# Adding products on constants to PSUM banks not yet in use, at four places of a linear-attention and mixer kernel

## The chip, the cores and the metric

One core of one Trainium2 chip runs the whole program. The metric is the device time of one execution in microseconds; the median over several executions counts. The engines are called by the names of the profile: PE (TensorE, matrix products and transposes), PEld (its weight loads), ACT (ScalarE), DVE (VectorE), POOL (GpSimd) and SP (SyncE, which issues the DMAs). PSUM is the memory that PE writes its results into; it has eight banks of 512 fp32 columns, and a pool hands them out under a tag.

## The reference

Linear attention over 4 batches of 8 heads, 576 positions, head width 64 and 128 features, then two mixer layers, each with a token mixing and a channel mixing:

```python
def phi(x):
    proj = np.einsum('bhsd,df->bhsf', x, w_phi)
    proj = proj - np.max(np.abs(proj), axis=-1, keepdims=True)
    return np.concatenate([np.exp(proj), np.exp(-proj)], axis=-1)
q_p, k_p = phi(q), phi(k)
kv = np.einsum('bhsf,bhsd->bhfd', k_p, v)
z = np.sum(k_p, axis=2)
num = np.einsum('bhsf,bhfd->bhsd', q_p, kv)
den = np.einsum('bhsf,bhf->bhs', q_p, z)[..., None] + 1e-06
x = (num / den)                     # then as (batch, seq, 512)
# first mixer (rank 32, hidden 2048)
u = x + (x.transpose(0, 2, 1) @ U @ V).transpose(0, 2, 1)
x = u + np.maximum(u @ w_ch1, 0) @ w_ch2
# second mixer (token width 256, hidden 1536)
u = x + (np.maximum(x.transpose(0, 2, 1) @ w_tok1, 0) @ w_tok2).transpose(0, 2, 1)
x = u + np.maximum(u @ w_ch1, 0) @ w_ch2
```

## The kernel before

The work is fp32. Most operands are split into a high part (`..h`) and the rest (`..l`), both in a rounded fp32 format that PE multiplies faster, and a product is the sum of high x high, high x low and low x high. `split` (lines 101 to 103) makes the two parts: one engine casts, another subtracts. The mixer weights come from memory as 64-bit floats; `load64` rebuilds an fp32 tile from the two words with two ACT steps (lines 138, 139) and two DVE steps (lines 141, 144), and `load_half` splits it, for `b` weights with a cast on ACT (`wh_b`, line 94) and a subtraction on POOL (`wl_b`, line 99).

The attention goes over 16 pairs of heads (`g`; four pairs make a batch): projections `pp`, exponentials, the sums over positions into `kvp`, four transposes `kvt` (function `k3`), ACT's cast of them to `KH`, then the products `nm` (function `q2`) of `KH` with the features of q. Pairs 0 to 3 are plain: they don't split q and k features (`g < NF32`). Function `proj` ends with two DVE steps on the projections, `km` and `kd`.

The first token mixing of a batch has three functions. `tm0` makes, for each of five position tiles, four transposes `xp` of the batch's `xT`, splits them to `xh` (ACT) and `xl` (DVE), and sums two products with the constant `US` into one bank, `rp`. `tm1` splits `rp` to `rh` (ACT) and `rl` (DVE). `tm2` makes the eight `mp` products, each of `rh` and of `rl` with the constant `VS`, which DVE adds to `xT` (line 445). After it `ma_u` splits `xT` to `uha` (ACT) and `ula` (DVE), and the first third of the channel mixing follows (`hp_a`, `yp`). The rest of the first channel mixing (`hp_b`, `yb`), the second token mixing of a batch (`tokmix2`: transposes `x2p`, parts `x2h` and `x2l`, sums `gp` with the constants `T1H` and `T1L`) and the second channel mixing (`hp_c`, `yc`) come behind that, with a new set of PSUM pools.

The code names these steps round by round (a table of rounds, `at`), but the order in which each engine gets its instructions is set by the scheduler of the tile framework: it takes the instructions of all engines, runs them against a timeline of its own and emits them in the order in which they come ready there. An engine works its own list strictly in that order; `issue_after(x)` forbids the scheduler to put an instruction ahead of `x`. PSUM pools during the attention and the first third of the first channel mixing: `psk`, one bank (tag `kvp`), `psx`, five banks, `psm`, two banks.

Of the kernel before, what the change touches and what calls it, by code (L numbers as in the profile page):

```python
# [8 lines left out]
F32 = mybir.dt.float32  # L9
# [10 lines left out]
P = 128  # L20
B = 4
# [3 lines left out]
F = 128  # L25
# [3 lines left out]
NT = 5  # L29
N = 288  # L30
# [7 lines left out]

NF32 = 4
WARM = 8  # L40


KQB = 6
# [44 lines left out]
def body(ctx, tc, kq, vd, w_phi, U, V, wm1, wt1, wt2, wm2, out):  # L88
    nc = tc.nc
# [13 lines left out]
        sub(el, lo, src, f32(hi))  # L103

    def mm(o, l, r, start, stop):
        nc.tensor.matmul(o, l, r, start=start, stop=stop, skip_group_check=True)  # L106

    def group(o, pairs, first=True):
        n = len(pairs)
        for i, (l, r) in enumerate(pairs):  # L110
            mm(o, l, r, first and i == 0, i == n - 1)

    cst = ctx.enter_context(tc.tile_pool(name="cst", bufs=1))
    dr = ctx.enter_context(tc.tile_pool(name="dr", bufs=1, space=DRAM))
# [4 lines left out]
    ident = cst.tile([P, P], F32, name="ident")  # L119
# [46 lines left out]
    def w2(w, c):  # L166
        return w[:, C + c * P : C + (c + 1) * P]

    def h_tile(pool, w, uh, ul, name, tag="m"):
        hp = pool.tile([P, 512], F32, tag=tag, name=f"hp_{name}")  # L170
        wh, wl = w
        g = []
        for c in range(NC):
            g += [(w1(wh, c), uh[:, c, :]), (w1(wh, c), ul[:, c, :]), (w1(wl, c), uh[:, c, :])]
        group(hp[:, : uh.shape[2]], g)
        return hp
# [13 lines left out]
    psk = PS.enter_context(tc.tile_pool(name="psk", bufs=1, space=PSUM))  # L190
# [26 lines left out]
    US = ac.tile([P, NT, 4, 32], F32R, name="US")  # L217
    VS = ac.tile([P, S], F32R, name="VS")
# [110 lines left out]
    def k3(g):  # L329
        kvT = a1.tile([P, 2, 2 * F], F32, tag="kvT", name=f"kvT{g}")  # L330
        cp("a", kvT, kvps.pop(g))
        tp = psx.tile([P, 4, P], F32, tag="x", name=f"kvt{g}")
        for j in range(2):
            for s in range(2):
                nc.tensor.transpose(tp[:, 2 * j + s, :], kvT[:, j, s * F : (s + 1) * F], ident)
        if g < NF32:
            KHs[g] = a2.tile([P, 4, P], F32, tag="KH", name=f"KH{g}")
            cp("a", KHs[g], tp)
            return
        KHs[g] = a2.tile([P, 4, P], F32R, tag="KH", name=f"KH{g}")  # L340
        KLs[g] = a2.tile([P, 4, P], F32R, tag="KL", name=f"KL{g}")
        split(tp, KHs[g], KLs[g], "a", "v")

    QT = ((0, 1, 4), (2, 3))
    QS = (slice(0, 320), slice(320, S))

# [23 lines left out]
    def q2(g, j, ch):  # L370
        nm = f"{g}_{j}_{ch}"
        n = QS[ch].stop - QS[ch].start
        eh, el = qe.pop((g, j, ch))
        ps = psx.tile([P, 512], F32, tag="x", name=f"nm{nm}")
        gr = [(KHs[g][:, 2 * j + s], eh[:, s]) for s in range(2)]
        if el is not None:
            gr += [(KLs[g][:, 2 * j + s], eh[:, s]) for s in range(2)]
            gr += [(KHs[g][:, 2 * j + s], el[:, s]) for s in range(2)]
        group(ps[:, :n], gr)
        if ch == 0:  # L380
            nds[g, j] = a1.tile([P, S], F32, tag=f"nd{j}", name=f"nd{g}_{j}")
        cp("a", nds[g, j][:, QS[ch]], ps[:, :n])
# [27 lines left out]
            for j, rows in enumerate((slice(0, D), slice(D, P))):  # L410
                nc.vector.tensor_mul(xTs[b][rows, hp, :], nds.pop((g, j))[rows], rec[rows])

    rps = {}

    def tm0(b, t):
        xT = xTs[b]
        if t == 0:
            rps[b] = psx.tile([P, C], F32, tag="x", name=f"rp{b}")
        rp = rps[b]
        r = P if t < 4 else D  # L420
        xp = psx.tile([P, C], F32, tag="x", name=f"xp{b}_{t}")
        for c in range(NC):
            nc.tensor.transpose(xp[:r, c * P : (c + 1) * P], xT[:, c, t * P : t * P + r], ident)
        xh = at2.tile([P, C], F32R, tag="xh", name=f"xh{b}_{t}")
        xl = at2.tile([P, C], F32R, tag="xl", name=f"xl{b}_{t}")
        split(xp[:r], xh[:r], xl[:r], "a", "v")
        us = US[:r, t].rearrange("p a r -> p (a r)")
        mm(rp, us, xh[:r], t == 0, False)
        mm(rp, us, xl[:r], False, t == NT - 1)

    def tm1(b):
        rh = at2.tile([P, C], F32R, tag="xh", name=f"rh{b}")
# [4 lines left out]
    def tm2(b, ch):  # L437
        rh, rl = rps[b]
        sl = slice(ch * N, (ch + 1) * N)
        xT = xTs[b]  # L440
        for c in range(NC):
            mp = psx.tile([P, 512], F32, tag="x", name=f"mp{b}_{ch}_{c}")
            cs = slice(c * P, (c + 1) * P)
            group(mp[:, :N], [(rh[:, cs], VS[:, sl]), (rl[:, cs], VS[:, sl])])
            nc.vector.tensor_add(xT[:, c, sl], mp[:, :N], xT[:, c, sl])
        nc.sync.dma_start(uD[2 * b + ch], xT[:, :, sl])

# [11 lines left out]
    wA = []  # L459
# [7 lines left out]
    uhl, hss = {}, {}  # L467
# [5 lines left out]
    def ma_h(b, ch, f):  # L473
        nm = f"a{b}_{ch}_{f}"
        pool, tag = (psx, "x") if b == B - 1 and f % 2 else (psm, "m")
        hp = h_tile(pool, wA[f], *uhl[b, ch], nm, tag)
        hh, hl = h_pair(f, nm)
        relu_split(hp[:, :N], hh, hl)
        hss[b, ch].append((hh, hl))
# [15 lines left out]
    for g in range(B * NPAIR):  # L495
        r = 5 * g
# [11 lines left out]
        for i in range(4):  # L508
            j, ch = i % 2, i // 2
# [67 lines left out]
    def tokmix2(b, x2):  # L577
        gp = [psg.tile([P, C], F32, tag=f"g{j}", name=f"gp{b}_{j}") for j in range(2)]
        for t in range(NT):
            r = P if t < 4 else D  # L580
            xp = psh.tile([P, C], F32, tag="m", name=f"x2p{b}_{t}")
            for c in range(NC):
                nc.tensor.transpose(xp[:r, c * P : (c + 1) * P], x2[:, c, t * P : t * P + r], ident)
            xh = b2.tile([P, C], F32R, tag="xh", name=f"x2h{b}_{t}")
            xl = b2.tile([P, C], F32R, tag="xl", name=f"x2l{b}_{t}")
            split(xp[:r], xh[:r], xl[:r], "a", "v")
# [125 lines left out]
```

## Time and profile before

| | us |
|---|---|
| median of 3 executions | 1081.95 |
| lowest, highest | 1081.44, 1084.78 |
| the profiled execution: own time | 1085.54 |
| its span (first to last instruction) | 1083.7 |
| PE busy | 1039.0 (96% of the span) |
| DVE, ACT, POOL busy | 575.2, 420.7, 226.2 |
| mean granted clock of PE, 1 being full | 0.983 |

The profiled execution is one of its own, beside the three. PE's share says that little of the span is left without a product or transpose; it doesn't say that they ran at full clock. The granted clock is therefore read with it, stretch by stretch. The stage of the last batch's token mixing lies at about 372 to 393 us, that of the plain pairs before 85, the second token mixing of the last batch at about 756 to 775.

### The profile page before, as it was taken

The page shows a single profiled execution, that of the slowest core. Times are in us where ns is not written, and L with a number is a line of the kernel's source. Part 1 is how long each engine was busy: PE and PEld are TensorE (multiplying, and loading weights), DVE is VectorE, ACT ScalarE, POOL GpSimd, SP SyncE. Part 2 cuts the span into 40 slices and gives each one's busy share as a digit, 9 for nine tenths or more (in the row PEclk, how much of TensorE's full clock was granted, in tenths as well). Part 3 has the DMA queues.
Part 4 walks back from the last instruction along what each step waited for, and adds up shares of the span by engine and source line. Part 5 has one row for each costly group of instructions (what it writes and reads, how often), then busy time and mean ns, then how long its engine had stood idle before and what let it go on. Part 6 is the DMA issues. An engine that isn't in the chain of part 4 may idle for free.

```text
span 1083.7 us, 16492 instructions
## 1 busy us (share of the span) xinstructions
PE 1039.0 (96%) x6528; PEld 945.5 (87%) x6528; DVE 575.2 (53%) x973; ACT 420.7 (39%) x953; POOL 226.2 (21%) x174
## 2 busy tenths in 40 slices
PE   8978899899989989999999999999999999999998
PEld 6757799789879879999999999999898888888886
DVE  6788987898898588743223223339941121211211
ACT  6676666665665477532112112127621111111110
POOL 3225565554545244200000000003200000000000
PEclk9998999999999969999999999999999999999999
DMA  7552313232220397520200200216401020020101
GB/s 213 151 150 66 97 56 92 75 92 71 75 83 16 110 304 230 176 79 22 88 23 22 88 22 23 88 39 202 150 23 60 1 77 1 1 77 1 39 1 38
DMA packets 59614, 87.36 MB, mean 81 GB/s; under 512 B 14353, under 2 KB 46353, under 8 KB 59537
## 3 DMA queue, kind: packets, MB, share of 16 engines
q1 hardware_dynamic: 59536, 86.32, 25.0%
q8 instruction: 51, 0.84, 0.3%
q14 instruction: 27, 0.21, 0.1%
HBM read 67.27 MB, written 18.95 MB: 80 GB/s over the span
## 4 chain that ended last, share of the span: by engine, by line
PE 79%; DVE 10%; ACT 4%; issue 3%; DMA 3%; POOL 1%; SPq 0%; DVEq 0%; POOLq 0%; ACTq 0%
PE hp_c L106 14%; PE yc L106 14%; PE yb L106 12%; PE hp_b L106 12%; PE hp_a L106 4%; PE pp L106 4%; PE yp L106 4%; PE kvp L106 3%; PE nm L106 3%; PE gp L106 3%; PE m2p L106 2%; PE dT L354 1%; DMA raw_a<-in_wm_dram 1%; DVE km L286 1%; POOL wl_b L99 1%
## 5 line engine op out<-in xcount | busy, mean ns | idle before, releaser
L180 DVE SCALAR_TENSOR_TENSOR hlc<-hp_c,hhc 128x504 fp32r<-128x504 f32 (+1 forms) x60 | 38.2, 636 | 225.4 <-ACT hhc L179 225.4
L179 ACT ACTIVATE hhc<-hp_c 128x504 fp32r<-128x504 f32 (+1 forms) x60 | 33.3, 556 | 247.8 <-PE hp_c L106 247.8
L180 DVE SCALAR_TENSOR_TENSOR hlb<-hp_b,hhb 128x288 fp32r<-128x288 f32 x88 | 40.1, 455 | 160.2 <-ACT hhb L179 160.2
L179 ACT ACTIVATE hhb<-hp_b 128x288 fp32r<-128x288 f32 x88 | 35.9, 408 | 198.2 <-PE hp_b L106 197.8
L106 PE MATMUL hp_b<-ulb,wh_b 128*128 128x288 f32 x352 | 104.0, 296 | 0.0
L106 PE MATMUL hp_b<-uhb,wl_b 128*128 128x288 f32 x352 | 104.0, 296 | 0.0
L106 PE MATMUL hp_b<-uhb,wh_b 128*128 128x288 f32 x352 | 103.8, 296 | 0.0
L106 PE MATMUL yb<-hlb,wh_b 128*128 128x288 f32 x352 | 97.4, 297 | 0.2 <-DVE hlb L180 0.2
L106 PE MATMUL yb<-hhb,wl_b 128*128 128x288 f32 x352 | 97.0, 295 | 0.0
L106 PE MATMUL hp_c<-ulc,wh_c 128*128 128x504 f32 (+1 forms) x240 | 89.1, 371 | 0.0
L106 PE MATMUL hp_c<-uhc,wl_c 128*128 128x504 f32 (+1 forms) x240 | 89.1, 371 | 0.0
L106 PE MATMUL hp_c<-uhc,wh_c 128*128 128x504 f32 (+1 forms) x240 | 88.5, 371 | 0.0
L106 PE MATMUL yc<-hlc,wh_c 128*128 128x504 f32 (+1 forms) x240 | 88.3, 371 | 0.0
L106 PE MATMUL yc<-hhc,wl_c 128*128 128x504 f32 (+1 forms) x240 | 88.1, 370 | 0.0
L99 POOL TENSOR_TENSOR wl_c<-w_c,wh_c 128x512 fp32r<-128x512 f32 x12 | 19.1, 1592 | 327.4 <-ACT wh_c L94 318.3
L99 POOL TENSOR_TENSOR qel<-qe,qeh 128x640 fp32r<-128x640 f32 (+1 forms) x48 | 71.5, 1501 | 26.5 <-ACT qeh L94 13.0
L106 PE MATMUL yc<-hhc,wh_c 128*128 128x504 f32 (+1 forms) x240 | 75.7, 371 | 0.0
L106 PE MATMUL yb<-hhb,wh_b 128*128 128x288 f32 x352 | 67.3, 296 | 1.6 <-ACT hhb L179 1.6
L106 PEld LDWEIGHTS hp_b<-uhb,wh_b 128*128 128x128 f32 x352 | 66.0, 188 | 1.2 <-PE gp L106 1.1
L106 PEld LDWEIGHTS yb<-hlb,wh_b 128*128 128x128 f32 x352 | 66.1, 188 | 1.0 <-DVE hlb L180 0.7
L106 PEld LDWEIGHTS hp_b<-ulb,wh_b 128*128 128x128 f32 x352 | 66.3, 188 | 0.1
L106 PEld LDWEIGHTS yb<-hhb,wl_b 128*128 128x128 f32 x352 | 66.3, 188 | 0.0
(181 smaller groups left out, 2793.1 us busy)
## 6 DMA issues: line engine op xcount, KB each, us to landing
raw_c<-in_wm_dram SPq DMA_DIRECT2D x24, 512.0 KB, 4.3
raw_b<-in_wm_dram SPq DMA_DIRECT2D x22, 512.0 KB, 5.1
kq<-in_kq_dram SPq DMA_DIRECT2D x80, 128.0 KB, 2.1
raw_a<-in_wm_dram SPq DMA_DIRECT2D x10, 512.0 KB, 4.4
rec<-rD SPq DMA_DIRECT2D x32, 144.0 KB, 3.1
uD<-xT SPq DMA_DIRECT2D x8, 576.0 KB, 3.5
sD<-xT SPq DMA_DIRECT2D x8, 576.0 KB, 4.7
ub<-uD SPq DMA_DIRECT2D x8, 576.0 KB, 3.7
```

The lines of the kernel that those rows point to most:

```text
L99: return ENG[e].tensor_tensor(out=o, in0=a, in1=b, op=ALU.subtract)
L106: nc.tensor.matmul(o, l, r, start=start, stop=stop, skip_group_check=True)
L179: nc.scalar.activation(hh, hp, AF.Relu)
L180: nc.vector.scalar_tensor_tensor(out=hl, in0=hp, scalar=0.0, in1=f32(hh), op0=ALU.max, op1=ALU.subtract)
L286: nc.vector.tensor_reduce(out=m, in_=pv, op=ALU.max, axis=AX.X, apply_absolute_value=True)
L354: nc.tensor.transpose(tp[:, o : o + r], ds["q", g, t][:r, j, :], ident[:r, :r])
```

## The change

A new helper, `keep(o, n, behind, r)`, issues n products of 128 x 128 columns of a constant on its own 512 columns (`US`, or `T1H`), all into PSUM tile `o`, and the scheduler may not put them ahead of the instruction `behind`. The result is read by no one: the first real product into the same bank overwrites it. There are 48 of them: 10 into the bank of the first `nm` of pair 3, behind the last `kvt` transpose; 6 into `mp0_0_0` and 6 into `mp3_0_0`, behind the batch's last `rp` product; 8, 2, 2, 2 and 2 into a bank of their own (`spare`, in the pool `psk`, whose bank is free by then), behind the five groups of transposes `xp3_t` of batch 3; 5 into the first `hp_a` of batch 3, behind its last `mp` product; 5 into `gp3_0`, behind the first `x2p` transposes of batch 3.

```diff
+KEEP_X = (8, 2, 2, 2, 2)
+KEEP_M = 6
+KEEP_U = 5
+KEEP_Q = 10
+KEEP_G = 5
     def mm(o, l, r, start, stop):
-        nc.tensor.matmul(o, l, r, start=start, stop=stop, skip_group_check=True)
-
-    def group(o, pairs, first=True):
+        return nc.tensor.matmul(o, l, r, start=start, stop=stop, skip_group_check=True)
+
+    def keep(o, n, behind, r=None):
+        r = US.rearrange("p t a r -> p (t a r)") if r is None else r
+        with tc.issue_after(behind):
+            for i in range(n):
+                mm(o, r[:, :P], r[:, :512], i == 0, i == n - 1)
+
+    def group(o, pairs, first=True, last=True):
...
         hp = pool.tile([P, 512], F32, tag=tag, name=f"hp_{name}")
+        if behind is not None:
+            keep(hp, KEEP_U, behind)
...
-                nc.tensor.transpose(tp[:, 2 * j + s, :], kvT[:, j, s * F : (s + 1) * F], ident)
+                kvl[g] = nc.tensor.transpose(tp[:, 2 * j + s, :], kvT[:, j, s * F : (s + 1) * F], ident).ins
...
         ps = psx.tile([P, 512], F32, tag="x", name=f"nm{nm}")
+        if g == NF32 - 1 and j == 0 and ch == 0:
+            keep(ps, KEEP_Q, kvl[g])
...
             rps[b] = psx.tile([P, C], F32, tag="x", name=f"rp{b}")
+            if b == B - 1:
+                spare.append(psk.tile([P, 512], F32, tag="kvp", name="spare"))
...
+        if b == B - 1:
+            keep(spare[0], KEEP_X[t], last)
...
-        mm(rp, us, xl[:r], False, t == NT - 1)
+        rpl[b] = mm(rp, us, xl[:r], False, t == NT - 1).ins
...
-            group(mp[:, :N], [(rh[:, cs], VS[:, sl]), (rl[:, cs], VS[:, sl])])
+            if c == 0 and ch == 0 and b in (0, B - 1):
+                keep(mp, KEEP_M, rpl[b])
+            group(mp[:, :N], [(rh[:, cs], VS[:, sl])], last=False)
+            mps[b] = mm(mp[:, :N], rl[:, cs], VS[:, sl], False, True).ins
...
-        hp = h_tile(pool, wA[f], *uhl[b, ch], nm, tag)
+        hp = h_tile(pool, wA[f], *uhl[b, ch], nm, tag, mps[b] if b == B - 1 and ch == 0 and f == 0 else None)
...
+            if b == B - 1 and t == 0:
+                keep(gp[0], KEEP_G, last, T1H.rearrange("p t j -> p (t j)"))
```

Since the scheduler works on all instructions at once, the added ones also change the order of others: on every engine from about the first `mp` products of batch 0 on to the middle of batch 1's attention (pairs 6 to 9 and the first channel mixing of batch 0 change places), and again in the stage of batch 3's token mixing. Up to pair 3's products the orders agree, and so they do between those stretches but for the numbers.

PE at the end of pair 3, before (the kernel's tile names with a running number; `x4` is four in a row):

```order
L335 MATMUL kvt3_840<-ident_77,kvT3_838 128x128 x4
L106 MATMUL nm3_0_0_847<-qf3_0_0_786,KH3_845 128x320 x2
L106 MATMUL nm3_1_0_852<-qf3_1_0_793,KH3_845 128x320 x2
L106 MATMUL pp4_1_861<-KWH_132,xgh4_1_857 128x256
L106 MATMUL pp4_1_861<-KWL_133,xgh4_1_857 128x256
```

and after (line 112 is the former 106, 349 the former 335):

```order
L349 MATMUL kvt3_840<-ident_77,kvT3_838 128x128 x4
L112 MATMUL nm3_0_0_847<-US_144 128x512 x10
L112 MATMUL nm3_0_0_847<-qf3_0_0_786,KH3_845 128x320 x2
L112 MATMUL nm3_1_0_862<-qf3_1_0_793,KH3_845 128x320 x2
L112 MATMUL pp4_1_871<-KWH_132,xgh4_1_867 128x256
```

Ten products have come between the transposes and the first `nm`; nothing else moved there.

PE in the token mixing of batch 3, behind the last product of `yp2_1_3`, before:

```order
L106 MATMUL rp3_4939<-xh3_0_4945,US_144 128x512
L423 MATMUL xp3_1_4951<-ident_77,xT3_4285 128x128 x4
L423 MATMUL xp3_2_4980<-ident_77,xT3_4285 128x128 x4
L423 MATMUL xp3_3_4991<-ident_77,xT3_4285 128x128 x4
L106 MATMUL rp3_4939<-xl3_0_4946,US_144 128x512
L423 MATMUL xp3_4_5002<-ident_77,xT3_4285 64x128 x4
L106 MATMUL rp3_4939<-xh3_1_4956,US_144 128x512
```

and after:

```order
L112 MATMUL rp3_4955<-xh3_0_4970,US_144 128x512
L442 MATMUL xp3_1_4976<-ident_77,xT3_4301 128x128 x4
L112 MATMUL spare_4956<-US_144 128x512
L112 MATMUL rp3_4955<-xl3_0_4971,US_144 128x512
L112 MATMUL spare_4956<-US_144 128x512
L442 MATMUL xp3_2_5007<-ident_77,xT3_4301 128x128 x4
L112 MATMUL spare_4956<-US_144 128x512 x2
L442 MATMUL xp3_3_5020<-ident_77,xT3_4301 128x128 x4
L112 MATMUL spare_4956<-US_144 128x512 x2
L442 MATMUL xp3_4_5033<-ident_77,xT3_4301 64x128 x4
L112 MATMUL spare_4956<-US_144 128x512 x2
L112 MATMUL rp3_4955<-xh3_1_4983,US_144 128x512
```

The small groups have come between the transposes; the eight of the first group stand further ahead, before the fifteen products of `yp2_1_3`. The six stand behind the last `rp` product, the five behind the last `mp` product, with nothing between them and the real products of their bank.

DVE in the same stage (lines 141 and 144 are the two steps of the weight conversion, 153 and 156 after; line 99, or 105, is the subtraction of a split), before:

```order
L141 SCALAR_TENSOR_TENSOR w_b0_1_5568<-w_b0_1_5568,r_b0_1_5569 128x512
L99 TENSOR_TENSOR xl3_1_4957<-xp3_1_4951,xh3_1_4956 128x512
L144 SCALAR_TENSOR_TENSOR w_b0_1_5568<-raw_b0_1_5566,w_b0_1_5568 128x512
L99 TENSOR_TENSOR xl3_2_4986<-xp3_2_4980,xh3_2_4985 128x512
L99 TENSOR_TENSOR xl3_3_4997<-xp3_3_4991,xh3_3_4996 128x512
L141 SCALAR_TENSOR_TENSOR w_b1_0_5580<-w_b1_0_5580,r_b1_0_5581 128x512
L99 TENSOR_TENSOR xl3_4_5008<-xp3_4_5002,xh3_4_5007 64x512
L144 SCALAR_TENSOR_TENSOR w_b1_0_5580<-raw_b1_0_5578,w_b1_0_5580 128x512
L141 SCALAR_TENSOR_TENSOR w_b1_1_5590<-w_b1_1_5590,r_b1_1_5591 128x512
L99 TENSOR_TENSOR rl3_5018<-rp3_4939,rh3_5017 128x512
```

and after:

```order
L105 TENSOR_TENSOR xl3_1_4984<-xp3_1_4976,xh3_1_4983 128x512
L153 SCALAR_TENSOR_TENSOR w_b1_0_5624<-w_b1_0_5624,r_b1_0_5625 128x512
L105 TENSOR_TENSOR xl3_2_5015<-xp3_2_5007,xh3_2_5014 128x512
L156 SCALAR_TENSOR_TENSOR w_b1_0_5624<-raw_b1_0_5622,w_b1_0_5624 128x512
L153 SCALAR_TENSOR_TENSOR w_b1_1_5634<-w_b1_1_5634,r_b1_1_5635 128x512
L156 SCALAR_TENSOR_TENSOR w_b1_1_5634<-raw_b1_1_5632,w_b1_1_5634 128x512
L105 TENSOR_TENSOR xl3_3_5028<-xp3_3_5020,xh3_3_5027 128x512
L105 TENSOR_TENSOR xl3_4_5041<-xp3_4_5033,xh3_4_5040 64x512
L153 SCALAR_TENSOR_TENSOR w_b2_0_5646<-w_b2_0_5646,r_b2_0_5647 128x512
L105 TENSOR_TENSOR rl3_5051<-rp3_4955,rh3_5050 128x512
```

Weight steps have moved ahead of the splits: `rl3` had the first step of `w_b1_1` before it, and has the first of `w_b2_0` now. From the first step of `w_b0_0` up to `ula3_0` DVE's list has ten weight steps before and thirteen after. On ACT the casts `xh3_3` and `xh3_4` stand behind `wh_b1_0` after, ahead of it before; on DVE, in the second token mixing of batch 3, `x2l3_0` stands ahead of the first two additions into `x2` and not behind them, and the first steps of `w_c7` ahead of `x2l3_1`, the second ones ahead of `x2l3_2`.

## Rows read from the trace of the kernel before

Times are microseconds; PE, DVE and so on are the engines. In the timelines a row is one instruction, or several alike in a row (x4), and the brackets hold the idle time of the engine just before it and who ended that.

**Rows 1.** The cores: span in us, mean granted clock of PE.

```profile
core 0: 1083.7 us, clock 0.983
```

**Rows 2.** The page: shares of the chain that ended last, by engine.

```profile
PE 79%; DVE 10%; ACT 4%; issue 3%; DMA 3%; POOL 1%; SPq 0%; DVEq 0%; POOLq 0%; ACTq 0%
```

**Rows 3.** Ten-us windows: busy us (instructions) of PE, PEld, DVE, ACT, POOL; PEclk; DMA.

```profile
70.00:80.00 10.00, 6.13 (x26) 4.19 (x25) 8.04 (x15) 6.54 (x17) 1.47 (x1) 0.86 0.58 166
90.00:100.00 10.00, 8.02 (x42) 7.72 (x43) 6.27 (x12) 4.53 (x13) 8.78 (x7) 0.66 0.30 86
380.00:390.00 10.00, 7.79 (x22) 5.32 (x23) 9.72 (x15) 7.28 (x12) 3.85 (x3) 0.55 0.80 270
390.00:400.00 10.00, 8.08 (x40) 7.73 (x41) 8.44 (x12) 6.65 (x12) 4.40 (x3) 0.60 1.02 336
760.00:770.00 10.00, 8.05 (x35) 6.25 (x34) 9.18 (x17) 6.24 (x11) 1.88 (x2) 0.83 0.41 138
```

**Rows 4.** PE timeline, pair 3: start, us, then line, tiles, count, wait before.

```profile
76.27 3.81 PE L106 MATMUL nm<-qf,KH 128*128 128x320 f32 x8 [3.34 <-ACT KH L94]
```

**Rows 5.** Window behind pair 3, columns as in rows 3.

```profile
76.70:83.50 6.80, 6.80 (x30) 5.42 (x29) 6.74 (x10) 3.25 (x9) 3.11 (x2) 0.75 0.58 174
```

**Rows 6.** DVE timeline behind that window.

```profile
84.00 1.40 DVE L286 TENSOR_REDUCE km<-pp 128x4 f32<-128x512 f32 x2 [0.49 <-PE pp L106]
```

**Rows 7.** PE timeline, token mixing of batch 0.

```profile
110.85 0.39 PE L106 MATMUL rp<-xl,US 128*128 128x512 f32 x1
111.08 0.39 PE L106 MATMUL rp<-xh,US 128*128 128x512 f32 x1
...
122.52 0.40 PE L106 MATMUL mp<-VS,rh 128*128 128x288 f32 x1 [2.20 <-DVE xT L445]
```

**Rows 8.** PE timeline, token mixing of batch 3.

```profile
375.40 0.51 PE L106 MATMUL rp<-xh,US 128*128 128x512 f32 x1 [0.81 <-ACT xh L94]
...
380.99 0.63 PE L106 MATMUL rp<-xh,US 128*128 128x512 f32 x1
381.42 0.63 PE L106 MATMUL rp<-xl,US 128*128 128x512 f32 x1
...
384.65 1.33 PE L106 MATMUL mp<-VS,rh 128*128 128x288 f32 x4 [0.68 <-ACT rh L94]
...
389.72 1.33 PE L106 MATMUL hp_a<-uha,wh_a 128*128 128x288 f32 x4 [0.47 <-ACT uha L94]
392.97 0.61 PE L106 MATMUL hp_a<-ula,wh_a 128*128 128x288 f32 x1 [1.92 <-DVE ula L99]
```

**Rows 9.** Window in the token mixing of batch 3, columns as in rows 3.

```profile
380.60:393.00 12.40, 8.87 (x26) 6.05 (x26) 12.12 (x19) 9.06 (x15) 4.40 (x4) 0.51 0.83 265
```

**Rows 10.** Windows of batch 3's hp_a products alone, columns as in rows 3 (no POOL).

```profile
393.00:398.00 5.00, 5.00 (x21) 5.00 (x22) 0.28 (x1) 0.40 (x1) 0.50 1.03 345
398.00:400.50 2.50, 2.50 (x21) 2.50 (x21) 0.17 (x1) 0.40 (x1) 1.00 1.07 410
```

**Rows 11.** DVE timeline, token mixing of batch 3.

```profile
376.11 0.68 DVE L144 SCALAR_TENSOR_TENSOR w_b<-raw_b,w_b 128x512 int32<-128x512 int32 x1
376.71 0.45 DVE L491 TENSOR_TENSOR xT<-yp,xT 128x288 f32<-128x288 f32 x1
...
378.28 1.69 DVE L144 SCALAR_TENSOR_TENSOR w_b<-raw_b,w_b 128x512 int32<-128x512 int32 x1
...
385.24 1.79 DVE L144 SCALAR_TENSOR_TENSOR w_b<-raw_b,w_b 128x512 int32<-128x512 int32 x1
```

**Rows 12.** POOL timeline, same stage.

```profile
378.15 1.28 POOL L99 TENSOR_TENSOR wl_b<-w_b,wh_b 128x512 fp32r<-128x512 f32 x1 [17.93 <-ACT wh_b L94]
```

**Rows 13.** PE timeline, second token mixing of batch 3.

```profile
756.97 0.79 PE L106 MATMUL yb<-hhb,wh_b 128*128 128x288 f32 x4 [0.45 <-ACT hhb L179]
...
762.26 0.50 PE L106 MATMUL gp<-x2l,T1H 128*128 128x512 f32 x1 [1.95 <-DVE x2l L99]
```

**Rows 14.** DVE timeline, same stage.

```profile
760.80 0.81 DVE L573 TENSOR_TENSOR x<-yb,x 128x288 f32<-128x288 f32 x2
```

More of the change, by code (lines that the diff above doesn't have):

```diff
@@ L105, in mm @@
     def mm(o, l, r, start, stop):
-        nc.tensor.matmul(o, l, r, start=start, stop=stop, skip_group_check=True)
-    def group(o, pairs, first=True):
+        return nc.tensor.matmul(o, l, r, start=start, stop=stop, skip_group_check=True)
[5 more added lines that the diff above has]
+    def group(o, pairs, first=True, last=True):
         n = len(pairs)
         for i, (l, r) in enumerate(pairs):
-            mm(o, l, r, first and i == 0, i == n - 1)
+            mm(o, l, r, first and i == 0, last and i == n - 1)
     cst = ctx.enter_context(tc.tile_pool(name="cst", bufs=1))
@@ L167, in w2, with h_tile @@
         return w[:, C + c * P : C + (c + 1) * P]
-    def h_tile(pool, w, uh, ul, name, tag="m"):
+    def h_tile(pool, w, uh, ul, name, tag="m", behind=None):
         hp = pool.tile([P, 512], F32, tag=tag, name=f"hp_{name}")
+        if behind is not None:
+            keep(hp, KEEP_U, behind)
         wh, wl = w
@@ L342, in k3 @@
         split(tp, KHs[g], KLs[g], "a", "v")
+    kvl = {}
     QT = ((0, 1, 4), (2, 3))
@@ L411, in x1 @@
                 nc.vector.tensor_mul(xTs[b][rows, hp, :], nds.pop((g, j))[rows], rec[rows])
-    rps = {}
+    rps, rpl, mps, spare = {}, {}, {}, []
     def tm0(b, t):
@@ L422, in tm0 @@
         for c in range(NC):
-            nc.tensor.transpose(xp[:r, c * P : (c + 1) * P], xT[:, c, t * P : t * P + r], ident)
+            last = nc.tensor.transpose(xp[:r, c * P : (c + 1) * P], xT[:, c, t * P : t * P + r], ident).ins
+        if b == B - 1:
+            keep(spare[0], KEEP_X[t], last)
         xh = at2.tile([P, C], F32R, tag="xh", name=f"xh{b}_{t}")
@@ L582, in tokmix2 @@
             for c in range(NC):
-                nc.tensor.transpose(xp[:r, c * P : (c + 1) * P], x2[:, c, t * P : t * P + r], ident)
+                last = nc.tensor.transpose(xp[:r, c * P : (c + 1) * P], x2[:, c, t * P : t * P + r], ident).ins
+            if b == B - 1 and t == 0:
+                keep(gp[0], KEEP_G, last, T1H.rearrange("p t j -> p (t j)"))
             xh = b2.tile([P, C], F32R, tag="xh", name=f"x2h{b}_{t}")
```

## Prediction, made before the changed kernel was run

> **What bounds the kernel now.** I read the cores first, then the chain, then the windows, then the timeline of the places that the change touches. The mean granted clock is 0.983 over a span of 1083.7 us [rows 1]: if every stretch below full speed were repaired, and TensorE (PE) set the end in all of them, that would give (1 - 0.983) x 1083.7 = 18.4 us, the ceiling for any change of this kind. The chain that ended last is PE for 79%, VectorE (DVE) for 10% [rows 2]: PE's work is on the path nearly everywhere, but some of it hands over to DVE. The windows show where PE is neither full nor at full clock [rows 3]: 70 to 80 us (0.86), 90 to 100 (0.66), 380 to 400 (0.55 and 0.60) and 760 to 770 (0.83). The change has products for the first, the third and the fourth; none stands before 90 to 100, whose 3.4 us at the most I leave as they are. A granted 0.50 is the lower of the two levels, 1.2 GHz instead of 2.4.
>
> So the question for each place is not whether PE gets busier, but two others: does the clock then stay at its upper level, and is PE what the next stage waits for.
>
> **A. Pair 3 (ten products).** PE waits 3.34 us for ScalarE's KH, then runs eight products at 76.27 in 3.81 us [rows 4]. Ten products of 512 columns at the spacing of the rp rows at full clock, 111.08 - 110.85 = 0.23 us [rows 7], are 2.3 us: they fit into the 3.34 and delay nothing. If the clock then stays up, the eight nm products take half of 3.81 and PE is 1.9 us earlier. Who uses that? DVE is busy for 6.74 of the 6.80 us from 76.7 on [rows 5], and PE's next projections need DVE's splits; DVE's first wait on PE after that is 0.49 us at 84.00 [rows 6]. What an earlier PE can give DVE is that 0.49. I take -0.5, bounds 0 (the clock falls all the same, or DVE stays full) and -1.9.
>
> **B. Batch 0 (six products) and what the scheduler made of it.** Six products stand ahead of mp0_0_0, 6 x 0.23 = 1.4 us, and the first real one needs only rh, long there. That delay is taken up behind it: after the first mp group PE waits 2.20 us for a DVE addition [rows 7]. More exposed is that between here and about 215 us all engines' orders changed: products of pairs 6 to 9 and of the first channel mix changed places. The trace of before cannot show what new waits that makes. I bound it by the one wait next to it, gone or once more: -2.2 to +2.2. The moved operations are the same ones, so I take 0.
>
> **C. Batch 3 (27 products, and DVE's order).** This is the largest term. From 380.6 to 393 DVE is busy 12.12 of 12.40 us [rows 9], and what ends the stage is DVE: at 392.97 PE waits 1.92 us for ula [rows 8]. The order shows ten steps of the weight conversion on DVE between the first, of w_b0_0, and ula before, and thirteen after. One that meets nothing lasts 0.68 and takes 0.60 of DVE's time (376.11 to the next at 376.71) [rows 11]. Three more are 3 x 0.60 = +1.8 us for ula. They are taken out of later work that DVE does beside a full PE, so nothing comes back for them.
>
> Against it stands the clock. The first 21 products of hp_a take 5.00 us at 0.50, the next 21 take 2.50 at 1.00 [rows 10]. In before the clock was down from about 381 on [rows 3], while PE waited 0.68 for rh, 0.47 for uha and 1.92 for ula [rows 8]; it rose at 398, after PE had worked from 393 without a gap [rows 10]. Now eight products fill the wait of 0.81 at 375.40, eight more stand between the transposes, six before mp, five before hp_a. The rp products still wait for xl as before, and the order puts xh3_3 and xh3_4 on ScalarE behind one more weight cast, so I expect the clock to fall near 381 again: nothing of the change fills that wait. But then six and five products at the half clock's spacing, 381.42 - 380.99 = 0.43 us [rows 8], are 2.6 and 2.2 us, and with the sixteen mp products between them PE works nearly without a gap from about 384 until ula comes. That is what it had done before the clock rose at 398, so I take the clock as up again when hp_a's row starts: -2.5. The 2.6 us ahead of mp cost little: DVE at that time works off weight steps. C is +1.8 - 2.5 = -0.7. Its ends: -2.5 if the three steps cost nothing, because DVE loses less to stalls; and upwards 3 x 1.79 = +5.4, with no gain from the clock, at the duration of the stalled step of 385.24 [rows 11].
>
> How likely that end is, rows tell too: the step at 378.28 lasted 1.69 instead of 0.68, having started 0.13 us behind GpSimd's wl_b of 1.28 us [rows 11, 12]. The Trainium skill has a rule for this, in SBUF - State Buffer, section "SBUF: two separate sides": DVE and GpSimd share a pair of ports as an exclusive lock, and the one that starts first holds it for its whole instruction (a DVE operation counts if it reads two operands from SBUF and GpSimd reads SBUF too). The rows agree with it: 1.28 - 0.13 + 0.60 is 1.75, and the step took 1.69. By that rule weight steps that are pulled into this stretch pull GpSimd's steps after them and are to be priced as stalled; the sum for C would then be +5.4 in place of -0.7.
>
> **D. Second token mixing, batch 3 (five products).** Behind x2p's transposes PE waits 0.45 us for hhb; five products are 5 x 0.23 = 1.15, so yb starts 0.7 us later. That lies ahead of a wait of 1.95 us for x2l at 762.26 [rows 13], which takes it up. x2l now stands on DVE ahead of the two additions that begin at 760.80 and last 0.81 together [rows 14], so it comes some 0.7 us sooner, while the next two x2l stand behind weight steps that stood after them. I take -0.6. If the clock also holds behind it, (1 - 0.83) x 10 = 1.7 us of the window come back [rows 3]: -1.7. If neither helps, +0.7.
>
> **The sum.** A -0.5, B 0, C -0.7, D -0.6: -1.8 us. The profiled execution took 1085.54 us, its span 1083.7 and 1.8 us around it; -1.8 makes 1083.7. The median of the three runs, 1081.95, lies 3.6 us below it, and the same difference on the median gives **1080.2 us**.
>
> **The rivals.**
> - The clock holds at all three places, and DVE has room: A -1.9, C -2.5, D -1.7, together -6.1, **1075.9 us**. For it: nothing but missing products keeps PE idle at pair 3 and in front of mp and hp_a. Against it: DVE is full at both places [rows 5, 9], and a PE that finishes earlier there only waits longer for DVE.
> - DVE's stalls in batch 3 decide: each of the three added weight steps meets a GpSimd step and lasts 1.79, the clock doesn't return before hp_a, since a later ula only makes PE wait longer. C is +5.4, the sum -0.5 + 5.4 - 0.6 = +4.3, **1086.3 us**, slower. It decides from the point where the three steps last more than (3.2 + 1.1) / 3 = 1.4 us each on average. For it: two of the ten steps lasted 1.69 and 1.79 [rows 11]. Against it: not every step can meet one, as GpSimd has one step for two of DVE's. This is the rival that the Trainium skill's rule of the exclusive lock leads to.
> - The products don't do what they are said to: the clock falls where it fell and comes back as late as before, and they stand ahead of work that is ready: 6 x 0.23 = 1.4 at mp0; in batch 3 8 x 0.23 - 0.81 = 1.0, 1.4 - 0.68 = 0.7 and DVE's 1.8; 1.15 - 0.45 = 0.7 at x2p. Together +5.6, **1087.6 us**. Against it: three of these have a wait behind them that swallows them.
>
> **How the numbers follow.** 0.3% is 3.2 us, about what a measurement of this kernel can tell from no change; the three runs of before spread over 3.3 us. The forecast (-1.8, with its terms free to move by some 3 us, 1078.7 to 1085.2) has 0.43, the first rival 0.35, the second 0.17 (with new waits in pairs 6 to 9, term B, in it), the third 0.05. Faster 0.35, same 0.43, slower 0.22. Both signs hold much, so the likeliest case's own range is 1078.7 to 1085.2; the range for 8 in 10 reaches to the first rival and just to the second: 1075.5 to 1086.5.
>
> **What would show it.** In the profile after: a granted clock near 1.00 in 76 to 81 us but DVE still full there, and a DVE that starts the split of ula some 2 us later than before, with thirteen weight steps ahead of it (C's cost); hp_a's first 21 products in 2.5 us instead of 5.00 (C's gain); weight steps of 1.7 us and more there speak for the second rival. The wait for x2l at 762.26 shorter than 1.95 shows D. The forecast is wrong if the clock stays up all through 375 to 398 and ula comes no later than before (first rival), or if it is down until 398 again (second or third); and B is wrong if PE's waits between 120 and 215 us in sum differ by more than 2.2 us.

## The result, and the profile after

| | before | after |
|---|---|---|
| median, us (executions) | 1081.44 (5) | 1088.58 (5) |
| lowest, highest | 1079.17, 1084.78 | 1085.66, 1091.89 |
| ratio to before, 95% interval | | 1.0067 [1.0045, 1.0089] |
| the profiled execution: own time, mean granted clock | 1085.54, 0.983 | 1085.66, 0.994 |

The changed kernel is slower by 0.67%, some 7 us. The forecast was 1080.2 us, and the measured time lies outside the range, above it. Here and below a loss in us is (ratio - 1) x 1082.

The cores and two lines of the page (busy time of the engines; the chain that ended last) say what the change did and didn't do:

```profile
core 0: 1083.9 us, clock 0.994
```

```profile
PE 1043.7 (96%) x6576; PEld 947.9 (87%) x6576; DVE 582.0 (54%) x973; ACT 420.7 (39%) x953; POOL 228.4 (21%) x174
...
PE 77%; DVE 12%; DMA 4%; issue 3%; ACT 2%; POOL 1%; SPq 0%; DVEq 0%; ACTq 0%; POOLq 0%
```

The clock was granted nearly everywhere, 0.994 against 0.983 [rows 1]. But DVE's share of the chain rose from 10% [rows 2] to 12%, and its 973 instructions, as many as before, took 582.0 us in place of 575.2. Both profiled executions are single ones and took the same time although the medians differ by 7 us: the one of before was a long one of its kind and the one of after the shortest of five. They are therefore compared by stretch. Windows of the changed kernel, columns as in rows 3:

```profile
70.00:80.00 10.00, 8.68 (x54) 7.31 (x52) 9.59 (x16) 6.26 (x20) 2.96 (x2) 1.00 0.49 162
90.00:100.00 10.00, 7.76 (x58) 6.89 (x57) 9.72 (x14) 7.17 (x21) 6.05 (x5) 1.00 0.23 67
380.00:390.00 10.00, 8.37 (x32) 6.59 (x31) 7.85 (x15) 6.71 (x10) 1.93 (x3) 0.75 0.70 239
390.00:400.00 10.00, 8.78 (x62) 8.31 (x62) 8.87 (x9) 5.61 (x12) 5.00 (x4) 1.00 1.00 360
400.00:410.00 10.00, 9.43 (x57) 9.20 (x58) 9.89 (x13) 7.09 (x14) 4.12 (x3) 0.83 0.51 187
760.00:770.00 10.00, 7.44 (x33) 4.91 (x33) 9.97 (x18) 6.54 (x11) 1.76 (x2) 1.00 0.41 144
```

Against [rows 3]: the clock is up in 70 to 80, 390 to 400 and 760 to 770, and half up in 380 to 390. It was also up in 90 to 100, where nothing had been put, and it was down in 400 to 410, where it had not been. What the stretches hand on is told by starts of the same instruction in two traces: the first `rp` of batch 3 began 5.4 us earlier after than before (369.97, 375.40), the first product of `hp_b` 0.25 us later. So whatever was ahead by 370 us had gone by 427. Much of that lead is no gain of the change: by pair 3's transposes, before the first added product, it was 4.9 us already (67.38, 72.27), from one execution to another. Some 3 us of that arose near 38 us, where PE waited 2.64 us for an exponential of ScalarE in the one and 1.20 in the other, and the eight products behind it took 3.64 us at the lower clock and 1.99 at the upper.

### The profile page after: what moved, and what is told of

The parts are those of the page before. It is cut to its first block, busy times and chain, and to the rows that moved or that the text cites. A ratio compares the mean times of both kernels' runs of the same rounds, so it can differ in the third digit from the quotient of the medians.

```text
span 1083.9 us, 16586 instructions
## 1 busy us (share of the span) xinstructions
PE 1043.7 (96%) x6576; PEld 947.9 (87%) x6576; DVE 582.0 (54%) x973; ACT 420.7 (39%) x953; POOL 228.4 (21%) x174
## 4 chain that ended last, share of the span: by engine, by line
PE 77%; DVE 12%; DMA 4%; issue 3%; ACT 2%; POOL 1%; SPq 0%; DVEq 0%; ACTq 0%; POOLq 0%
PE hp_c L112 14%; PE yc L112 14%; PE hp_b L112 12%; PE yb L112 12%; PE yp L112 5%; PE hp_a L112 4%; PE pp L112 3%; PE kvp L112 3%; PE m2p L112 2%; PE nm L112 2%; PE gp L112 2%; PE dT L369 1%; DVE xT L428 1%; DVE km L300 1%; DMA raw_b<-in_wm_dram 1%
```

## The experiments

Sixteen runs, each in five rounds beside the kernel before.

### Which of the four places

Each of the first four kernels keeps the added products of one place and drops the others, as in the first:

```diff
-        if b == B - 1:
-            keep(spare[0], KEEP_X[t], last)
...
-            if c == 0 and ch == 0 and b in (0, B - 1):
+            if c == 0 and ch == 0 and b in ():
...
-            if b == B - 1 and t == 0:
-                keep(gp[0], KEEP_G, last, T1H.rearrange("p t j -> p (t j)"))
```

Pair 3:

> The kernel before with the ten products of pair 3 alone; the order of all other instructions is that of before. The prediction's step A: -0.5 us (0 to -1.9). If the loss of the changed kernel came from the attention's part, this or the next kernel would have to be slower by several us; the traces say it isn't, so 1079 to 1083, within 0.3% of before.

Batch 0:

> The kernel before with the six products ahead of batch 0's first mp alone; with them the scheduler changes the order of all engines in pairs 6 to 9, as in the changed kernel. Theory O (the loss lies in batch 3's stage): no change, within 2 us of before. Rival theory B (the new order of pairs 6 to 9 costs): +3 us or more.

Batch 3:

> The kernel before with the 27 products of batch 3's token mixing alone; DVE's and ScalarE's order in that stage is that of the changed kernel (thirteen weight steps ahead of ula). In the two traces the changed kernel loses 6.2 us between 349 and 427 us. Theory O: the whole loss is here, +5 to +7 us. Rival theory B: less than +3 us.

Second token mixing:

> The kernel before with the five products of the last second token mixing alone, with the order that they bring. The two traces differ by 0.26 us there: +0.3 us, at the most 1 us to either side. The prediction's step D said -0.6.

| kernel | ratio [95%] | us |
|---|---|---|
| pair 3 alone | 0.9987 [0.9970, 1.0004] | -1.4 |
| batch 0 alone | 1.0025 [1.0010, 1.0040] | +2.7 |
| batch 3 alone | 1.0064 [1.0040, 1.0087] | +6.9 |
| second token mixing alone | 1.0012 [0.9996, 1.0027] | +1.3 |

Batch 3 carries the loss, batch 0 a smaller one. Batch 0's alone is no clean number for its own place: with it the scheduler changed the order of the `hp_a` stage of batch 3 as well, which took 1.0 us longer in its trace than before.

### The products or the order

Two things came with the change: products, and a new order on every engine. They can be parted: a table, made from the built program of before or of the changed kernel, pins every engine's list to that order (an issue order, no wait). The kernels of this and the next two sections have this edit and differ in the table, and in whether the products are in.

```diff
+ORDER = "..."
+def fix_order(tc, kept, first):
...
+    for eng, steps in json.loads(zlib.decompress(base64.b85decode(ORDER))).items():
...
+                if prev is not None:
+                    tc.add_manual_dep(i, prev.name, NoSync, reason="order")
+                prev = i
```

Products of batch 3, old order:

> The 27 products of batch 3's token mixing alone, as in the third kernel, but every engine's list of instructions is pinned to that of the kernel before, and the products stand directly behind the instruction that they were put behind. Theory O (the new order of DVE and ScalarE costs the time, the products none): no loss, -3 to +1 us against before. Theory P (the products stand in the way of ready ones, six of them at half clock ahead of mp: 2.7 us in the trace): +2 to +4 us.

New order, no products:

> The kernel before without any added product, with every engine's list pinned to the order of the changed kernel. Theory O: it carries the whole loss and more, +7 to +10 us, since nothing holds the clock. Theory P: +3 us or less.

All products, old order:

> All 48 products, every engine's list pinned to the order of before (batch 0's six stand directly ahead of their bank's first real product). Theory O: faster than before, -1 to -6 us, with the gain of pair 3 (-2.3 measured alone) in it. Theory P: +1 to +4 us.

The last of them once more:

> All 48 products with every engine's list pinned to the order of before, once more, since its gain of 0.2% lay close to what can be told: -1 to -4 us against before again if it is one.

| kernel | ratio [95%] | us |
|---|---|---|
| batch 3's products, old order | 1.0002 [0.9984, 1.0021] | +0.2 |
| new order, no products | 1.0079 [1.0060, 1.0098] | +8.5 |
| all products, old order | 0.9980 [0.9965, 0.9995] | -2.2 |
| the same again | 0.9991 [0.9970, 1.0011] | -1.0 |

This settles the main question. **The order alone costs as much as the whole change (+8.5 [+6.5, +10.6] and +7.2 [+4.9, +9.6] us), and the products in the old order cost nothing**; they gain a little, the first time clear of noise, the second time not. Starts in the traces, against the starts before (375.40, 384.65 and 392.97 in [rows 8]), show where:

| start, less the start before | after | products of batch 3, old order | order alone | all products, old order |
|---|---|---|---|---|
| first `rp` of batch 3 | -5.43 | +0.50 | -0.90 | -5.52 |
| first `mp` | -1.77 | +2.86 | +1.30 | -3.46 |
| first product with `ula` | -2.52 | +1.51 | +1.52 | -5.09 |
| first `hp_b` | +0.25 | +1.47 | +4.59 | -5.14 |

From the first `rp` to `ula` the changed kernel loses 2.9 us, the order alone 2.4, the kernels in the old order 1.0 and 0.4. From `ula` to `hp_b` it is 2.8 and 3.1, and the kernels in the old order neither lose nor gain there: 33.73 and 33.72 us, before 33.77.

### Which part of the order

> No added products. The order of the changed kernel up to the last batch's first transposes (pairs 6 to 9 with the first channel mixing of batch 0), the order of before from there on. In the trace of the order alone this stretch loses 3.2 us between 119 and 209 us, in that of the changed kernel 1.8: +2 to +3 us. If the loss of that stretch was chance: within 1 us.

> No added products. The order of the changed kernel in batch 3's token mixing alone, from the first split up to ula (thirteen weight steps on DVE ahead of it, casts of weights ahead of xh on ScalarE); the order of before elsewhere. The prediction's price of the three steps: +1.8 us; by the trace of the order alone +2.4. If ula's delay is made good behind it: 0.

> No added products. The order of before up to ula of batch 3, that of the changed kernel from there to the start of hp_b (weight steps among the splits of hp_a); nothing of that was priced in the prediction. By the trace of the order alone +3.1 us. If only ula's delay counts: 0.

| new order only in (no products) | ratio [95%] | us |
|---|---|---|
| pairs 6 to 9 | 1.0009 [0.9992, 1.0026] | +1.0 |
| batch 3 up to `ula` | 1.0033 [1.0012, 1.0055] | +3.6 |
| batch 3 behind `ula` | 1.0062 [1.0039, 1.0084] | +6.7 |

The three add up to more than the order alone (8.5), within their intervals, and the last two overlap. The kernel with the new order behind `ula` alone has the ten weight steps of before ahead of `ula`, so the three that the changed kernel does there stand behind it: six weight steps between `ula` and the first split `hla` of `hp_a`, where before has four and the changed kernel three. From the first product with `ula` to the first of `hp_b` its trace has 40.8 us, the changed kernel's 36.5, before's 33.8. So +6.7 is not the price of this stretch in the changed kernel; there it is the 2.8 to 3.1 us above.

Behind `ula` PE had been dense before. PE there, in the kernel with the new order behind `ula` alone, and beside it the rows of DVE and ScalarE that the wait of 2.14 us goes back to:

```profile
402.34 0.40 PE L138 MATMUL hp_a<-uha,wh_a 128*128 128x288 f32 x1 [2.14 <-DVE hla L213]
```

```profile
399.55 0.69 DVE L174 SCALAR_TENSOR_TENSOR w_b<-w_b,r_b 128x512 int32<-128x512 int32 x1 [1.88 <-ACT w_b L171]
400.27 1.65 DVE L177 SCALAR_TENSOR_TENSOR w_b<-raw_b,w_b 128x512 int32<-128x512 int32 x1
401.84 0.45 DVE L213 SCALAR_TENSOR_TENSOR hla<-hp_a,hha 128x288 fp32r<-128x288 f32 x1
```

```profile
398.85 0.67 ACT L171 ACTIVATE w_b<-raw_b 128x512 f32<-128x512 f32 x1 [1.76 <-POOL wl_b L131]
...
400.84 0.39 ACT L212 ACTIVATE hha<-hp_a 128x288 fp32r<-128x288 f32 x1
```

The split that PE waits for, `hla`, takes 0.45 us on DVE at 401.84. It stands behind two weight steps. The first of them had waited 1.88 us for ScalarE's `w_b`, which had waited 1.76 for GpSimd to give a buffer free, and the second took 1.65 instead of 0.68. ScalarE's half, `hha`, stands behind the same weight at 400.84. In the order of before, DVE did that split at 397.72, ahead of these two:

```profile
397.11 0.69 DVE L144 SCALAR_TENSOR_TENSOR w_b<-raw_b,w_b 128x512 int32<-128x512 int32 x1
397.72 0.45 DVE L180 SCALAR_TENSOR_TENSOR hla<-hp_a,hha 128x288 fp32r<-128x288 f32 x1
```

In the changed kernel itself the waits behind `ula` are shorter. The longest two are at the first `yp` products; beside them stand rows of DVE and GpSimd:

```profile
399.21 0.40 PE L112 MATMUL yp<-hla,wh_a 128*128 128x288 f32 x1 [0.51 <-DVE hla L194]
...
400.36 0.54 PE L112 MATMUL yp<-hha,wh_a 128*128 128x288 f32 x2 [0.62 <-ACT hha L193]
```

```profile
397.11 1.68 DVE L156 SCALAR_TENSOR_TENSOR w_b<-raw_b,w_b 128x512 int32<-128x512 int32 x1
398.71 0.44 DVE L194 SCALAR_TENSOR_TENSOR hla<-hp_a,hha 128x288 fp32r<-128x288 f32 x1
```

```profile
396.94 1.30 POOL L105 TENSOR_TENSOR wl_b<-w_b,wh_b 128x512 fp32r<-128x512 f32 x1 [2.42 <-ACT wh_b L100]
```

There the split `hla` is late less by the number of weight steps ahead of it than by their length: up to the fifth `hla` behind `ula` nine steps take 10.9 us, in before eight take 7.9. The one at 397.11 began while GpSimd's `wl_b` of 396.94 ran.

Three kernels test the reading that splits come late behind weight steps. The first two move steps in the order behind `ula`, the third only exchanges DVE's list:

> No added products. The order of the changed kernel behind ula, as in the kernel before this one that lost 6.7 us with it, but the five splits of the first hp_a row (hha on ScalarE, hla on DVE) put back behind the same weight steps as in before. Theory H (a split stands behind a weight step that itself waits for its buffer, and PE waits for the split): most of the loss of that stretch goes, +1 to +3 us against before. Rival theory W (simply more weight work on DVE within the stretch, wherever the splits stand): +5 us or more stays.

> No added products. As the kernel with the changed order behind ula, but every step of DVE and ScalarE there that is not of the weight conversion (hla, hha, the next ula and uha, the additions into xT) put behind as many weight steps as in before; PE's and SyncE's lists stay those of the changed kernel. Theory: what PE waits for next stands behind weight steps on DVE, so that putting back the first row alone only moved the loss to the next such step. Then the loss goes: within 2 us of before. If PE's or SyncE's list carries it: +4 us or more.

> No added products, the order of before on every engine but DVE, whose list behind ula is that of the changed kernel. If DVE's list carries the loss behind ula: +4 to +7 us. If it is ScalarE's and SyncE's: within 2 us of before.

| kernel (no products) | ratio [95%] | us |
|---|---|---|
| first row's splits put back | 1.0066 [1.0039, 1.0093] | +7.1 |
| all splits and additions put back | 1.0036 [1.0014, 1.0058] | +3.9 |
| DVE's list alone exchanged | 1.0125 [1.0100, 1.0150] | +13.5 |

DVE's list alone cost twice what was expected, so it can't be read as DVE's share of the loss. The first came out with the number of theory W, but not in its way: in its trace the first row lost nothing any more, and as much was lost at the next two places where PE waits for DVE:

```profile
412.07 0.40 PE L138 MATMUL hp_a<-ula,wh_a 128*128 128x288 f32 x1 [1.04 <-DVE ula L131]
...
414.84 0.40 PE L138 MATMUL hp_a<-uha,wh_a 128*128 128x288 f32 x1 [2.24 <-DVE xT L524]
```

```profile
409.06 1.69 DVE L177 SCALAR_TENSOR_TENSOR w_b<-raw_b,w_b 128x512 int32<-128x512 int32 x1
410.67 1.34 DVE L131 TENSOR_TENSOR ula<-xT,uha 128x1152 fp32r<-128x1152 f32 x1
412.01 1.69 DVE L174 SCALAR_TENSOR_TENSOR w_b<-w_b,r_b 128x512 int32<-128x512 int32 x1
...
414.34 0.82 DVE L524 TENSOR_TENSOR xT<-yp,xT 128x288 f32<-128x288 f32 x2
```

`ula` of the second half came behind a weight step of 1.69 us, and PE's next wait, 2.24 us, was for the addition into `xT` at 414.34, behind two more. With all of these steps put back the loss is +3.9, between the two expectations; its interval overlaps that of +6.7, so the times alone don't show that any of it went. The traces do: from `ula` to `hp_b` it is 37.1 us, about half of the way from 40.8 back to 33.8, and the eight traces with the old order there and in the stretch ahead of it lie within 33.7 to 34.2. The rest wasn't separated: in that kernel PE still waits 1.44 us for an `hla` that stands behind a stalled weight step, and what differs from before is only the order of two weight steps on DVE, of some casts on ScalarE, and PE's and SyncE's lists, which remain a rival for this half. ScalarE's list alone was not exchanged.

```profile
414.22 0.40 PE L138 MATMUL hp_a<-uha,wh_a 128*128 128x288 f32 x1 [1.44 <-DVE hla L213]
```

```profile
412.13 1.67 DVE L177 SCALAR_TENSOR_TENSOR w_b<-raw_b,w_b 128x512 int32<-128x512 int32 x1
413.72 0.81 DVE L213 SCALAR_TENSOR_TENSOR hla<-hp_a,hha 128x288 fp32r<-128x288 f32 x2
```

### Two variants of the pinned kernel

> All 48 products in the order of before, as in the kernel with everything pinned (-2.5 us), and besides two weight steps of DVE that stand ahead of ula in batch 3 moved directly behind it. If DVE's steps ahead of ula set the start of hp_a's row, and the work behind has room for them: another -1.2 to -1.8 us, -3.5 to -4.5 against before. If DVE behind ula has no room, as the stretch behind ula in the changed kernel suggests: no gain over the pinned one, or a loss.

Measured 1.0000 [0.9983, 1.0018]: no gain, and 1 to 2 us worse than the pinned kernel's two results, within the intervals. `ula` came after a wait of 0.74 us instead of 1.92 [rows 8], but the two steps now stood ahead of the first `hla`:

```profile
389.60 0.40 PE L144 MATMUL hp_a<-ula,wh_a 128*128 128x288 f32 x1 [0.74 <-DVE ula L137]
...
398.00 0.61 PE L144 MATMUL hp_a<-uha,wh_a 128*128 128x288 f32 x1 [2.28 <-DVE hla L228]
```

```profile
395.93 1.65 DVE L190 SCALAR_TENSOR_TENSOR w_b<-raw_b,w_b 128x512 int32<-128x512 int32 x1
397.50 0.45 DVE L228 SCALAR_TENSOR_TENSOR hla<-hp_a,hha 128x288 fp32r<-128x288 f32 x1
```

Two steps of DVE are all that differs from the pinned kernel here: from the first `rp` to `ula` the trace gains 1.2 us (16.8 for 18.0), from `ula` to `hp_b` it loses 2.7 (36.5 for 33.7).

> The pinned kernel with all products but the six ahead of batch 3's mp (42 products, order of before). In the pinned kernel's trace these six ran at the half clock and mp began 2.1 us later relative to the first rp product than before, while hp_a's row behind it ran faster. If they cost more than they bring: -1 to -2 us beside the pinned kernel, -3.5 to -4.5 against before. If they bring the clock back: the pinned kernel's gain shrinks to 0 to -1.5.

```diff
-            if c == 0 and ch == 0 and b in (0, B - 1):
+            if c == 0 and ch == 0 and b == 0:
```

Measured 0.9998 [0.9981, 1.0015]. It lies on the side of "they bring the clock back", but the interval reaches into those of the pinned kernel, so by the times what the six products are worth stays open. In the traces they delay `ula` by 0.3 to 1.0 us (0.1 us later than before without them, 0.4 to 1.1 with them), and bring nothing by `hp_b` (33.7 us from `ula` on either way).

## Why the prediction was wrong

**Where it failed: the new order was priced at two places and by one number, and the clock's return was booked as time gained.** Batch 3 alone, term C, was forecast at -0.7 us and measured +6.9 [+4.3, +9.4]. Two steps of it failed.

The first is the order behind `ula`. The prediction saw that the scheduler had sorted the work anew. It gave that 0 for pairs 6 to 9 (term B) and +1.8 us for three weight steps ahead of `ula` (in term C), and put the rest at nothing with one sentence: the three steps "are taken out of later work that DVE does beside a full PE, so nothing comes back for them". Behind `ula`, PE is full only as long as DVE's splits come in time. The new order reaches further than the text ahead of the prediction says, to 425 us of before's trace on PE and 454 on DVE, and made the splits late: 2.8 us from `ula` to `hp_b` in the trace of the changed kernel, 3.1 in that of the order alone. No row of before could have priced it: the orders behind `ula` were not compared.

The second is the -2.5 for the clock: it came back, and nothing of that was left by `hp_b` (below).

**B**: taken as 0 within 2.2. Pairs 6 to 9 in the new order measured +1.0 [-0.9, +2.8], which leaves both 0 and the bound open. In the traces the stretch from batch 0's first `rp` to batch 1's takes 96.7 to 97.7 us in the four with the new order there, 94.9 to 96.0 in the fourteen with the old one, 1.8 more on average: within the bound, but 0 was too low.

**C, the order up to `ula`**: +1.8 was forecast, +3.6 [+1.3, +6.0] measured for it, 2.4 from the first `rp` to `ula` in its trace, but not by the cause named. Windows of the `w_b` instructions alone, from DVE's first one to `ula` and from there to `hp_b`, before and after (the busy columns are DVE, ACT, POOL):

```profile
374.90:391.50 16.60, 10.05 (x10) 5.67 (x9) 5.13 (x4) 0.68 0.69 222
391.50:426.70 35.20, 18.88 (x22) 13.71 (x22) 14.84 (x11) 0.91 0.78 260
```

```profile
368.90:389.00 20.10, 9.57 (x13) 7.05 (x11) 7.16 (x5) 0.83 0.65 215
389.00:427.00 38.00, 21.87 (x21) 12.74 (x21) 15.61 (x11) 0.96 0.73 248
```

The thirteen steps ahead of `ula` took 9.57 us, the ten of before 10.05. DVE wasn't busier there, it waited:

```profile
373.32 0.69 DVE L105 TENSOR_TENSOR xl<-xp,xh 128x512 fp32r<-128x512 f32 x1 [0.81 <-ACT xh L100]
...
379.58 1.30 DVE L153 SCALAR_TENSOR_TENSOR w_b<-w_b,r_b 128x512 int32<-128x512 int32 x1 [0.77 <-ACT w_b L150]
...
384.32 0.82 DVE L469 TENSOR_TENSOR xT<-mp,xT 128x288 f32<-128x288 f32 x2 [2.15 <-PE mp L112]
```

```profile
376.33 0.62 ACT L100 CAST wh_b<-w_b 128x512 fp32r<-128x512 f32 x1 [0.53 <-DVE w_b L156]
376.86 1.05 ACT L100 CAST xh<-xp 128x512 fp32r<-128x512 f32 x2
```

0.81 us for `xh`, 0.77 for a weight and 2.15 for `mp`, where it had been busy for 12.12 of 12.40 us [rows 9]. `xh` was late because ScalarE's casts of weights stood ahead of it, and the one at 376.33 waited itself for DVE. PE's rows show both delays, and the six products ahead of `mp`:

```profile
369.97 0.39 PE L112 MATMUL rp<-xh,US 128*128 128x512 f32 x1
...
377.49 0.50 PE L112 MATMUL rp<-xh,US 128*128 128x512 f32 x1 [1.23 <-ACT xh L100]
...
380.16 2.93 PE L112 MATMUL mp<-US 128*128 128x512 f32 x6
382.88 1.16 PE L112 MATMUL mp<-VS,rh 128*128 128x288 f32 x4
...
388.09 0.79 PE L112 MATMUL hp_a<-uha,wh_a 128*128 128x288 f32 x4 [0.24 <-ACT uha L100]
390.45 0.40 PE L112 MATMUL hp_a<-ula,wh_a 128*128 128x288 f32 x1 [1.57 <-DVE ula L105]
```

**C, the clock**: it came back as forecast, but the gain did not. The clock fell in that stretch (380 to 390 at 0.75), was up again before `hp_a`'s row, and 20 products of it took 2.75 us instead of some 5 at the half clock [rows 10]:

```profile
390.40:393.20 2.80, 2.75 (x20) 2.75 (x21) 0.00 (x0) 0.41 (x1) 1.00 0.96 278
```

PE was 2.2 us ahead of before by the end of that row, counted from its first product with `ula`. At the first `yp` products it waited for `hla` and `hha` (399.21 and 400.36 above), the clock fell again (400 to 410 at 0.83), and the lead was gone. The old order shows the same. With batch 3's products in it the row ran at the full clock from its start, and then PE waited for `hla`, here and once more at 424.77, where before had no wait (a window of the `hp_a` products alone, and PE's row):

```profile
394.48:397.20 2.72, 2.72 (x20) 2.72 (x21) 0.00 (x0) 0.00 (x0) 1.00 1.01 338
```

```profile
406.25 0.40 PE L144 MATMUL yp<-hla,wh_a 128*128 128x288 f32 x1 [0.39 <-DVE hla L228]
```

The stretch from `ula` to `hp_b` took 33.73 us, before 33.77 with the row at the half clock. So the -2.5 was worth nothing there: DVE's splits set that stretch, not PE. The prediction had this argument, against its own first rival ("a PE that finishes earlier there only waits longer for DVE"), and did not apply it to C.

That the six products ahead of `mp` "cost little" did not hold: at half clock they took 2.7 us to the first `mp`, while ScalarE had begun `rh` at 380.27 and needed 0.59 for it; DVE, which was to work off weight steps meanwhile, waited 2.15 us. With batch 3's products in the old order `mp` came 2.4 us later against the first `rp`, `ula` 1.0, and `hp_b` still 1.0; the whole kernel measured +0.2 [-1.7, +2.3].

**A** has the right sign: -1.4 [-3.2, +0.4] measured, with the -0.5 in the interval, and no gain as well. From pair 3's transposes to the first `rp` of batch 0 the six traces with these products take 32.2 us on average, the twelve without 33.9: -1.6, nearer the bound of -1.9. The products took 2.54 us of the wait, and `nm` ran at full clock, eight in 2.42 us instead of 3.81 [rows 4]:

```profile
67.79 2.54 PE L112 MATMUL nm<-US 128*128 128x512 f32 x10
71.42 2.42 PE L112 MATMUL nm<-qf,KH 128*128 128x320 f32 x8 [1.08 <-ACT KH L100]
```

**D** was wrong: +1.3 [-0.4, +2.9] for -0.6. The first step was right, `x2l` came 0.85 us earlier (762.26 before), and the clock held. But the next one came 0.4 us later than before (764.89), behind the weight steps that had passed it; the forecast had named them and given them no price. From the first `x2p` to the first `hp_c` the three traces with this order have 14.7 to 14.8 us, before 14.5: +0.3.

```profile
761.41 0.50 PE L112 MATMUL gp<-x2l,T1H 128*128 128x512 f32 x1 [1.22 <-DVE x2l L105]
...
765.27 0.50 PE L112 MATMUL gp<-x2l,T1H 128*128 128x512 f32 x1 [0.87 <-DVE x2l L105]
```

By these stretches, each of single executions, the change makes -1.6 (A), +1.8 (B), +2.9 and +2.8 (C), +0.3 (D): +6.2, of the 7.2 [4.9, 9.6] measured.

**The rivals.** The first, 1075.9 us, came nearer with the clock, which held at pair 3 and behind `x2p` and came back in batch 3; it failed on its condition that DVE has room. The second, with the right sign and 1086.3 us, put the loss on weight steps that meet GpSimd's ahead of `ula`. Its place was wrong: the thirteen steps there took no longer than the ten. Behind `ula` they did, 21 steps with 21.87 us against 22 with 18.88. That is its mechanism in another place. How a step comes to be long, the traces show without exception: in all eighteen, each of the 261 `w_b` steps over 0.8 us began while a step of GpSimd ran, and none of the 531 shorter ones did. The exclusive lock of the Trainium skill (SBUF - State Buffer, "SBUF: two separate sides") agrees with that. That every step moved would meet one, as the +5.4 for C took it, the traces don't bear out: 15 of 44 did in the changed kernel, 14 of 44 before. (The prediction counted two long ones among the ten ahead of `ula`; there are four, of 1.69, 1.30, 1.79 and 1.18 us.) The page's row of busy time for two kernels with the same 973 instructions on DVE, the order alone and all products in the old order, shows what it adds up to:

```profile
PE 1040.4 (96%) x6528; PEld 945.3 (87%) x6528; DVE 582.6 (54%) x973; ACT 421.3 (39%) x953; POOL 228.4 (21%) x174
```

```profile
PE 1041.0 (97%) x6576; PEld 948.2 (88%) x6576; DVE 572.8 (53%) x973; ACT 420.2 (39%) x953; POOL 225.6 (21%) x174
```

582.6 us, against 575.2 in before: 7 us more for nothing but another order; and 572.8 with the products in the old one. The third rival, that the products stand in the way, is refuted: of its +5.6 the products make 3.8, and in the old order they cost nothing.

Without the order, the prediction's A and the clock of C make -3.0; the kernel with all products in the old order measured -2.2 and -1.0 (1080.24 and 1081.04 us, before beside them 1082.74 and 1082.78). That is near by number and not by reason: from `ula` to `hp_b` it gains nothing, and what it gains the traces show at pair 3. That 1080.2 was forecast for the changed kernel is chance. This kernel is clearly faster than the changed one, and faster than before in the first set of runs; in the second the interval holds no change.

## What to carry to other kernels

When a scheduler sets the order, an added instruction is two changes: run the new order without the instructions and the instructions in the old order before either is judged. Price a new order where PE waits for nothing too: see for each split or addition that PE needs next which steps now stand ahead of it on its engine, whether those wait for a buffer themselves, and whether they now run beside steps of another engine that make them longer. A clock that is granted again is worth something only where the next stage isn't waiting for another engine.

## What the runs showed that was not expected

- The mean granted clock rose in a kernel that got 0.67% slower: from 0.983 to 0.994 in the profiled executions, from 0.985 to 0.991 on average over 122 and 5.
- Order alone moved DVE's busy time for the same instructions from 575.2 to 582.6 us.
- A `w_b` step of DVE took 0.67 to 0.70 us, or 1.01 to 1.79 when GpSimd was at work as it began: 792 steps in eighteen traces, no exception.
- DVE's list exchanged alone, with the other engines as before, cost 13.5 us: lists that were sorted together don't fit one by one.
- Two executions with the same order and the same instructions up to there reached pair 3's transposes 4.9 us apart (72.27 and 67.38), most of it from one wait of PE for ScalarE near 38 us and the lower clock behind it.
